# Decode attention over 65,536 keys: the last sixteen slots of V summed straight into the result, with idle matmuls ahead of the last piece

## The chip, the cores and the metric

The kernel runs on one core of one Trainium2 chip. The metric is the device time of one execution in microseconds (us). A profile is one traced execution. Its span is about 2 us shorter than the time of that execution (633.7 against 635.62 us in `before`).

## The reference, cut to what matters

```
q: [1, 32, 1, 128]   k, v: [1, 8, 65536, 128]   all bf16
scores = q . k^T * 128**-0.5        # each of the 8 heads of k and v serves 4 of q
p      = softmax(scores)            # over 65536 keys
out    = p . v                      # [1, 32, 1, 128]
```

K and V together are 268.4 MB and each element has to be read once, so the task is to read them.

## The kernel before: the parts that the change touches

The keys of one head are loaded in four steps of 4 MB. A step holds T = 128 *slots*: one slot is 128 keys, one on each partition, with 128 columns of V. The last step of the last head is loaded in five pieces, so that TensorE can begin on the first while the others are on their way:

```python
    CUTS = (T // 2, 3 * T // 4, 7 * T // 8, T - T // 16)     # 64, 96, 112, 120
    EDGE = CUTS[-1]                                          # 120
    # ... (v_step, collect and store: cut)
    def last_step(g, j):
        vt = load(v_view[g, j], "vt", CUTS)
        E = E_tiles.pop(g)
        Dp = psm.tile([P, D], fp32, name="Dp", tag="misc")
        nc.vector.memset(Dp[:, :], 0.0)

        def slot(t, dst, start, stop):
            i, c = t // CW, t % CW
            nc.tensor.matmul(
                out=dst, lhsT=E[:, j, c, i * HPG:(i + 1) * HPG],
                rhs=vt[:, t * D:(t + 1) * D], start=start, stop=stop,
            )

        ps_f = collect(g, False)
        for t in range(EDGE):
            s = t % NQ
            slot(t, Dp[s * QP:s * QP + HPG, :], t < NQ, t >= EDGE - NQ)
        Ds = stats.tile([P, D], fp32, name="Ds")
        nc.vector.tensor_copy(out=Ds[:, :], in_=Dp[:, :])
        for t in range(EDGE, T):
            slot(t, ps_f[:, :], False, False)
        nc.tensor.matmul(
            out=ps_f[:, :], lhsT=selh[:, :], rhs=Ds[:, :], start=False, stop=True
        )
        store(g, ps_f, nc.sync)       # scale by 1/sum on VectorE, then the output DMA
```

`vt` is the loaded part of V, `E` the exponentials of the scores, `HPG` the 4 rows of q that a head serves, and `Z`, below, a constant tile that holds q. There are two ways for a slot. Into `Dp`, four neighbouring slots go to four groups of partitions, and they overlap in the timeline below: eight take 0.28 us, where one takes 0.22 us. Into `ps_f`, the result itself, all go to the same 4 partitions and follow one another, 55 ns apart: eight take 0.61 us. What lies in `Dp` is copied (to `Ds`, 0.29 us on VectorE) and folded into the result by one fp32 matmul with `selh`, which the trace shows as two passes (`x2`, 0.38 us from the start of the first to the end of the second). Below, "piece 4" is slots 112 to 119, and "the last piece" is slots 120 to 127.

## Time and profile before

| | before |
|---|---|
| time, median of the first 3 runs | 635.18 us (635.05 to 635.27) |
| span of the profiled execution | 633.7 us |
| TensorE / VectorE busy | 59% / 54% |
| mean rate of DMA over the span | 424 GB/s |

The page of the profile of before, first its line of busy times, then from the table of 40 slices the share of DMA in tenths, then the chain of waits by engine:

```profile
PE 376.3 (59%) x2314; PEld 151.0 (24%) x2314; DVE 344.5 (54%) x342; ACT 21.7 (3%) x25; POOL 4.9 (1%) x7
...
DMA  9999999999999999999999999999999999999995
...
DMA 70%; PE 12%; DVE 9%; issue 7%; ACT 1%; ACTq 0%; DVEq 0%
```

DMA is busy in every slice but the last. No compute engine is busy for more than 59% of the span, and this change works behind the last landings only, so what it can gain lies there. The chain of waits from 600 us on (start, duration, what) shows how short that part is:

```profile
600.07 30.08 DMA vt<-in_v_dram
630.14 0.04 issue
630.19 0.61 PE ps_f L238 x8
630.79 0.23 PE ps_f L251 x2
631.02 0.03 issue
631.05 0.34 DVE o L225
```

The same stretch in the timeline (start, duration, engine, line, operation, output<-inputs, shapes, count, and in brackets the idle time before it and what ended it):

```profile
628.88 0.40 PE L238 MATMUL Dp<-vt,E 128*4 128x128 bf16 x16 [0.63 <-DMA vt<-in_v_dram]
...
629.55 0.28 PE L238 MATMUL Dp<-vt,E 128*4 128x128 bf16 x8 [0.28 <-DMA vt<-in_v_dram]
...
629.88 0.29 DVE L248 COPY Ds<-Dp 128x128 f32<-128x128 f32 x1 [5.30 <-PE Dp L238]
630.19 0.61 PE L238 MATMUL ps_f<-vt,E 128*4 128x128 bf16 x8 [0.36 <-DMA vt<-in_v_dram]
...
630.63 0.38 PE L251 MATMUL ps_f<-Ds,selh 128*4 128x128 f32 x2
631.05 0.34 DVE L225 TENSOR_SCALAR o<-ps_f,rl 4x128 bf16<-4x128 f32 x1 [0.88 <-PE ps_f L251]
```

Each group of slots waits for its own piece. Piece 4 lands at 629.55 and the last piece 0.64 us later. (I take the start of a piece's first slot for its landing; the chain puts the end of the DMA itself 0.04 us before it.) From there the path is: eight slots in a row, two passes of `selh`, the scaling. The yardstick is the time **from slot 112 (piece 4's landing) to the start of VectorE's scaling**. It is 1.50 us here (631.05 - 629.55).

### The profile page before, as it was taken

The page shows a single profiled execution, that of the slowest core. Times are in us where ns is not written, and L with a number is a line of the kernel's source. Part 1 is how long each engine was busy: PE and PEld are TensorE (multiplying, and loading weights), DVE is VectorE, ACT ScalarE, POOL GpSimd, SP SyncE. Part 2 cuts the span into 40 slices and gives each one's busy share as a digit, 9 for nine tenths or more (in the row PEclk, how much of TensorE's full clock was granted, in tenths as well). Part 3 has the DMA queues.
Part 4 walks back from the last instruction along what each step waited for, and adds up shares of the span by engine and source line. Part 5 has one row for each costly group of instructions (what it writes and reads, how often), then busy time and mean ns, then how long its engine had stood idle before and what let it go on. Part 6 is the DMA issues. An engine that isn't in the chain of part 4 may idle for free.

```text
span 633.7 us, 5456 instructions
## 1 busy us (share of the span) xinstructions
PE 376.3 (59%) x2314; PEld 151.0 (24%) x2314; DVE 344.5 (54%) x342; ACT 21.7 (3%) x25; POOL 4.9 (1%) x7
## 2 busy tenths in 40 slices
PE   0696846785457745477544775547664476644825
PEld 0232312231122311133211332113221132211313
DVE  0899834774338753376533765437554375553600
ACT  0000100010000000010000100001000010000100
POOL 3000000000000000000000000000000000000000
PEclk9999888877788967789677986779976799767867
DMA  9999999999999999999999999999999999999995
GB/s 366 430 429 429 430 435 434 429 430 435 431 429 432 430 429 430 433 434 431 431 432 427 430 432 430 429 430 434 429 431 429 432 429 430 431 432 432 429 424 232
DMA packets 10071, 268.82 MB, mean 424 GB/s; under 512 B 1344, under 2 KB 1344, under 8 KB 1728
## 3 DMA queue, kind: packets, MB, share of 16 engines
q1 hardware_dynamic: 9800, 268.44, 98.7%
q8 instruction: 18, 0.29, 0.2%
q10 hardware_dynamic: 248, 0.04, 0.0%
q14 instruction: 5, 0.04, 0.0%
HBM read 268.47 MB, written 0.01 MB: 424 GB/s over the span
## 4 chain that ended last, share of the span: by engine, by line
DMA 70%; PE 12%; DVE 9%; issue 7%; ACT 1%; ACTq 0%; DVEq 0%
DMA kt<-in_k_dram 56%; DMA vt<-in_v_dram 12%; PE S L136 8%; DVE kT L128 8%; DMA q_85<-in_q_dram 2%; DVE mx L147 1%; PE ps_f L216 1%; ACT ET L167 1%; PE A_1900 L200 0%; PE A_772 L200 0%; PE A_773 L200 0%; PE A_1901 L200 0%; DVE Z L112 0%; PE A_396 L200 0%; ACTq L77 0%
## 5 line engine op out<-in xcount | busy, mean ns | idle before, releaser
L136 PE MATMUL S<-kT,Z 128*128 128x512 bf16 x1024 | 283.9, 429 | 207.8 <-DVE kT L128 200.8
L128 DVE STREAM_TRANSPOSE kT<-kt 128x1024 int32<-128x1024 int32 x256 | 292.2, 1207 | 209.0 <-DMA kt<-in_k_dram 208.0
L136 PEld LDWEIGHTS <-Z 128*128 128x128 bf16 x1024 | 108.2, 106 | 381.5 <-issue 300.1
L200 PEld LDWEIGHTS <-E 128*32 128x32 bf16 x992 | 25.1, 100 | 49.4 <-issue 29.6
L167 ACT ACTIVATE ET<-S,nm 128x2048 bf16<-128x2048 f32 x8 | 15.7, 1967 | 575.2 <-DVE nm L164 575.2
L147 DVE TENSOR_REDUCE mx<-S 128x1 f32<-128x2048 f32 x8 | 18.3, 2292 | 10.4 <-PE S L136 10.4
L172 DVE STREAM_TRANSPOSE E<-ET 128x2048 bf16<-128x2048 bf16 x8 | 18.5, 2309 | 3.2 <-ACT ET L167 3.2
L200 PE MATMUL A_2977<-vt,E 128*32 128x512 bf16 x48 | 6.8, 544 | 13.6 <-DMA vt<-in_v_dram 13.6
L213 DVE COPY As_3088<-A_2978 128x512 f32<-128x512 f32 x1 | 0.7, 692 | 22.4 <-PE A_2978 L200 22.4
L149 PE MATMUL ps_t<-ident,mx 128*1 128x128 f32 x8 | 2.3, 283 | 16.9 <-DVE mx L147 16.9
L102 DVE STREAM_TRANSPOSE qT<-q_85 128x64 int32<-128x64 int32 x1 | 0.2, 246 | 16.4 <-DMA q_85<-in_q_dram 16.4
L200 PE MATMUL A_2652<-vt,E 128*32 128x512 bf16 x64 | 8.1, 426 | 0.0
L200 PE MATMUL A_2653<-vt,E 128*32 128x512 bf16 x64 | 7.9, 421 | 0.0
L200 PE MATMUL A_397<-vt,E 128*32 128x512 bf16 x64 | 7.4, 409 | 0.0
L175 PE MATMUL ps_l<-ls,selh 128*4 128x1 f32 x16 | 1.5, 165 | 9.9 <-ACT ET L167 9.9
L200 PE MATMUL A_396<-vt,E 128*32 128x512 bf16 x64 | 7.4, 401 | 0.0
L200 PE MATMUL A_2276<-vt,E 128*32 128x512 bf16 x64 | 7.0, 382 | 0.2 <-DMA vt<-in_v_dram 0.2
L200 PE MATMUL A_1148<-vt,E 128*32 128x512 bf16 x64 | 6.9, 382 | 0.0
L200 PE MATMUL A_1524<-vt,E 128*32 128x512 bf16 x64 | 6.9, 382 | 0.0
L200 PE MATMUL A_1900<-vt,E 128*32 128x512 bf16 x64 | 6.9, 382 | 0.0
L200 PE MATMUL A_772<-vt,E 128*32 128x512 bf16 x64 | 6.9, 382 | 0.0
L200 PE MATMUL A_2978<-vt,E 128*32 128x512 bf16 x48 | 6.9, 548 | 0.0
(95 smaller groups left out, 106.1 us busy)
## 6 DMA issues: line engine op xcount, KB each, us to landing
kt<-in_k_dram SPq DMA_DIRECT2D x32, 4096.0 KB, 46.1
vt<-in_v_dram SPq DMA_DIRECT2D x31, 4096.0 KB, 39.9
vt<-in_v_dram SPq DMA_DIRECT2D x1, 2048.0 KB
vt<-in_v_dram SPq DMA_DIRECT2D x1, 1024.0 KB
vt<-in_v_dram SPq DMA_DIRECT2D x1, 512.0 KB
vt<-in_v_dram SPq DMA_DIRECT2D x2, 256.0 KB
out_dram<-o ACTq DMA_DIRECT2D x7, 1.0 KB
q_85<-in_q_dram ACTq DMA_DIRECT2D x4, 8.0 KB, 6.5
```

The lines of the kernel that those rows point to most:

```text
L102: nc.vector.transpose(out=qT[:, :].bitcast(i32), in_=q4[:, :].bitcast(i32))
L128: nc.vector.transpose(out=kT[:, :].bitcast(i32), in_=kt[:, i * CW * D:(i + 1) * CW * D].bitcast(i32),)
L136: nc.tensor.matmul(out=S[:, j, :NCOL], lhsT=Z[:, b, e, g, w0:w0 + P], rhs=kT_v[:, b, e, :, :], start=(i == 0 and be == 0), stop=(i == NI - ...
L147: nc.vector.reduce_max(out=mx[:, :], in_=S[:, :, :NCOL], axis=AX.XY)
L149: nc.tensor.transpose(out=ps_t[:, :], in_=mx[:, :], identity=ident[:, :])
L167: nc.scalar.activation(out=ET[:, :].rearrange("p (a n) -> p a n", a=NQ), in_=S[:, :, :NCOL], func=ACT.Exp, bias=nm[:, :], scale=SCALE, acc ...
L172: nc.vector.transpose(out=E[:, :, :, :].rearrange("p a c r -> p (a c r)"), in_=ET[:, :])
L175: nc.tensor.matmul(out=ps_l[:, :], lhsT=selh[:, :], rhs=ls[:, :], start=True, stop=True)
L200: nc.tensor.matmul(out=A[u][s * QP:(s + 1) * QP, :], lhsT=E[:, j, c, :], rhs=vt_v[:, u, c, :, :], start=(j == 0 and c0 == 0), stop=(j == e ...
L213: nc.vector.tensor_copy(out=As[1][:, :, :].rearrange("p i d -> p (i d)"), in_=A[1][:, :])
L216: nc.tensor.matmul(out=ps_f[:, :], lhsT=sel[:, i * HPG:(i + 1) * HPG], rhs=As[i // HI][:, i % HI, :], start=(i == 0), stop=(stop and i == ...
```

## The change

Its intent: take the `selh` matmul out of the path behind the last landing. For that, the copy `Ds` has to come one piece sooner, so piece 4 goes straight into the result as well. Three idle matmuls, whose output nobody reads, are put where TensorE waits for the last piece, to keep it busy.

```diff
-    CUTS = (T // 2, 3 * T // 4, 7 * T // 8, T - T // 16)
-    EDGE = CUTS[-1]
+    CUTS = (T // 2, 3 * T // 4, 7 * T // 8, 15 * T // 16)    # the same numbers
+    EDGE = CUTS[-2]                                          # 112 instead of 120
 ...
+        W = psa.tile([P, 2 * D], fp32, name="W", tag="A0")
 ...
-        for t in range(EDGE, T):
+        def idle_work(n):
+            for _ in range(n):
+                nc.tensor.matmul(
+                    out=W[:, :], lhsT=Z[:, 0, 0, 0, :P],
+                    rhs=vt[:, (CUTS[-1] - 2) * D:CUTS[-1] * D], start=True, stop=True,
+                )
+
+        for t in range(EDGE, CUTS[-1]):
             slot(t, ps_f[:, :], False, False)
         nc.tensor.matmul(
-            out=ps_f[:, :], lhsT=selh[:, :], rhs=Ds[:, :], start=False, stop=True
+            out=ps_f[:, :], lhsT=selh[:, :], rhs=Ds[:, :], start=False, stop=False
         )
+        idle_work(3)
+        for t in range(CUTS[-1], T):
+            slot(t, ps_f[:, :], False, t == T - 1)
         store(g, ps_f, nc.sync)
```

The A tiles also get the tags that they already had by name, so that `W` can take the first one's place. (The comments after `#` are mine.)

More of the change, by code (lines that the diff above doesn't have):

```diff
@@ L189, in v_step @@
             A_tiles[g] = [
-                psa.tile([P, HI * D], fp32, name=f"A{u}") for u in range(2)
+                psa.tile([P, HI * D], fp32, name=f"A{u}", tag=f"A{u}") for u in range(2)
             ]
```

## The prediction

> **What bounds the kernel.** The DMA stream. The slice table shows DMA at 9 tenths or more in every slice but the last, 424 GB/s over the span, 268.44 MB; the chain of waits puts 70% of the span on DMA of K and V. In the last chain, DMA of V runs from 600.07 to 630.14 us; after it come only 0.61 us of eight matmuls on the last piece, 0.23 us of the two-pass selh matmul, a 0.34 us VectorE scaling at 631.05, and the output DMA issued at 631.42 (span 633.7). So the change can touch about 0.9 us of 635: 0.14%.
>
> **What changes.** The pieces of the load stay the same (120 = 15*128/16). Only TensorE's tail is reordered: slots 112 to 119 leave Dp for ps_f, the copy Ds moves ahead one piece, the selh matmul moves from behind the last piece to before it, and three 256-column idle matmuls stand between it and the last eight slots.
>
> **Costs, from the timeline of before (TensorE's granted clock was 1.00 from 628.8 to 631.1).**
> - Gap of two slots into ps_f: starts 630.19 to 630.52 in six steps, 55 ns. [...]
> - The selh matmul: two passes, 110 ns apart (630.63, 630.74), so about 0.22 us of TensorE's time. This leaves the path behind the last piece: the intended gain.
> - Slots 112 to 119 in Dp use four column groups (eight in 0.28 us, start to last end); in ps_f they follow one another at 55 ns: eight take about 0.44 us. That is 0.37 us more of TensorE's issue time before the last piece.
> - Ds: the 16 slots of the third piece end near 629.28, the copy takes 0.29 us, ready near 629.65: before selh needs it.
>
> **The sum.** Piece four released TensorE at 629.55, the last piece at 630.19. After: slots 112-119 issue from 629.55 to 629.99, selh to 630.21[...]. The last piece has then been there for about 0.35 us. The last eight slots start at about 630.54 and the last one at 630.93, with its end near 631.15 (218 ns each). Before, the last selh pass ended at 631.01. So the gain of 0.22 us is given back by 0.35 us of work standing in the way: the idle matmuls do not fill a wait, they overrun it. Net +0.1 us if the pieces land 0.64 us apart as here; -0.2 us if the last piece lands 0.4 us or more later. TensorE was already at clock 1.00 here, so warming buys nothing.
>
> **Predicted:** 635.2 us, 8 in 10 within 634.5 to 635.8. Faster by over 2%: 0.003; within 2%: 0.994; slower: 0.003.
>
> **What would show it.** DMA at 430 GB/s and the same landing times. The last eight slots not released by the DMA of V but by the PE queue (no idle time before them); TensorE's wait for the last piece, 0.36 us before, gone; VectorE's scaling at about 631.2 rather than 631.05. If the intent worked, the slots would idle until the DMA, and the scaling come 0.22 us sooner after it.
>
> **What would make it wrong.** Pieces landing further apart than in this one trace (then up to 0.2 us faster); the copy Ds or W's bank holding selh or the idle matmuls up; weight loads of the idle matmuls that are not hidden; or the whole DMA stream running differently in that program or session, which moves more than any of these terms.

The sum came to the last eight slots at about 630.54, 0.99 us after slot 112, and to net +0.1 us. The step from 630.21 (the end of `selh`) to 630.54 is the 0.33 us that it gave to the three idle matmuls. That was the estimate, and the 0.35 us, 630.93 and 631.15 that follow rest on it. `e2_idle24` later measured 0.110 us for each further idle matmul.

## The result, and the profile after

| | before | changed |
|---|---|---|
| median of 6 runs each | 635.43 us (635.05 to 635.85) | 635.56 us (635.27 to 635.79) |
| ratio | | 1.0001 (95% interval 0.9988 to 1.0014) |
| slot 112 to the scaling, first profile | 1.50 us | 1.84 us |

Ratios here are the mean time of one kernel's fast runs over that of the other's fast runs of the same rounds, so they are not quite the ratio of the medians. The time is the same. The profile shows that the two tails are not. Timeline of the changed kernel:

```profile
629.05 0.29 DVE L249 COPY Ds<-Dp 128x128 f32<-128x128 f32 x1 [4.74 <-PE Dp L238]
629.27 0.61 PE L238 MATMUL ps_f<-vt,E 128*4 128x128 bf16 x8 [0.28 <-DMA vt<-in_v_dram]
...
629.72 0.38 PE L259 MATMUL ps_f<-Ds,selh 128*4 128x128 f32 x2
...
630.03 0.50 PE L252 MATMUL W<-vt,Z 128*128 128x256 bf16 x3
...
630.46 0.61 PE L238 MATMUL ps_f<-vt,E 128*4 128x128 bf16 x8
631.11 0.34 DVE L225 TENSOR_SCALAR o<-ps_f,rl 4x128 bf16<-4x128 f32 x1 [1.77 <-PE ps_f L238]
```

And the chain of waits, in order of time:

```profile
629.27 0.61 PE ps_f L238 x8
629.88 0.22 PE ps_f L259 x2
630.10 0.43 PE W L252 x3
630.53 0.55 PE ps_f L238 x8
```

The last eight slots carry no bracket: TensorE did not idle before them, and no DMA released them. The chain that ended last runs through the idle matmuls. The last eight slots start 1.19 us after slot 112, where before they started after 0.64 us. The scaling, counted from piece 4, comes 0.34 us later than before. In absolute time it is only 0.06 us later (631.11 against 631.05), because piece 4 happened to land 0.28 us sooner in this execution.

### The profile page after: what moved, and what is told of

Same layout as the page of the kernel before. It is cut to its first block, busy times and chain, and to the rows that moved or that the text cites. A ratio compares the mean times of both kernels' runs of the same rounds, so it can differ in the third digit from the quotient of the medians.

```text
span 633.8 us, 5462 instructions
## 1 busy us (share of the span) xinstructions
PE 382.8 (60%) x2317; PEld 153.8 (24%) x2317; DVE 344.8 (54%) x342; ACT 21.7 (3%) x25; POOL 4.9 (1%) x7
## 4 chain that ended last, share of the span: by engine, by line
DMA 70%; PE 12%; DVE 10%; issue 7%; ACT 0%; SPq 0%; ACTq 0%; DVEq 0%
DMA kt<-in_k_dram 56%; DMA vt<-in_v_dram 12%; PE S L136 8%; DVE kT L128 8%; DMA q_85<-in_q_dram 2%; DVE mx L147 1%; PE A_396 L200 0%; PE A_397 L200 0%; PE A_773 L200 0%; DVE E L172 0%; PE A_772 L200 0%; ACT ET L167 0%; DVE Z L112 0%; SPq L72 0%; ACTq L77 0%
## 5 line engine op out<-in xcount | busy, mean ns | idle before, releaser
L136 PE MATMUL S<-kT,Z 128*128 128x512 bf16 x1024 | 289.8, 441 | 200.8 <-DVE kT L128 196.0
L136 PEld LDWEIGHTS <-Z 128*128 128x128 bf16 x1024 | 110.3, 108 | 378.2 <-issue 299.3
```

The lines of the kernel that those rows point to most:

```text
L136: nc.tensor.matmul(out=S[:, j, :NCOL], lhsT=Z[:, b, e, g, w0:w0 + P], rhs=kT_v[:, b, e, :, :], start=(i == 0 and be == 0), stop=(i == NI - ...
```

## The experiments

Two theories at the start. **A**: TensorE's order of work decides. The serial slots, `selh` and the idle matmuls together take longer than the 0.64 us between the last two landings, and the clock does not matter. **B**: the idle matmuls are of use, as they keep TensorE's clock up. A third possibility, **C**, was that the last piece simply landed late in the changed kernel's profile. The second profile of before brought a further theory, **W**, which comes below.

### The change without its idle matmuls (e1_idle0)

```diff
-        idle_work(3)
+        idle_work(0)
```

> The change without its three idle matmuls. Theory A (the idle matmuls and the serial slots overrun the last piece; the clock does not matter): from the first of slots 112-119 to VectorE's scaling, 1.50 us before and 1.84 us in the changed kernel, becomes 1.2 to 1.35 us; the last eight slots start 0.65 to 0.75 us after slot 112 instead of 1.19; the granted clock of 628 us on stays 1.00 and the slots follow at 55 ns. Rival B (the idle matmuls keep TensorE fast): the last slots follow at more than 55 ns and the clock is below 1.00. Rival C (the last piece simply landed late in the changed kernel's run): the last eight slots still start about 1.19 us after slot 112. Time: the same as before within 0.1%, since 0.2 us is 0.03%.

Measured: 635.33 us, ratio 0.9996 (0.9983 to 1.0008), correct. Timeline:

```profile
629.36 0.61 PE L238 MATMUL ps_f<-vt,E 128*4 128x128 bf16 x8 [0.28 <-DMA vt<-in_v_dram]
...
629.80 0.38 PE L259 MATMUL ps_f<-Ds,selh 128*4 128x128 f32 x2
...
630.02 0.61 PE L238 MATMUL ps_f<-vt,E 128*4 128x128 bf16 x8
630.67 0.34 DVE L225 TENSOR_SCALAR o<-ps_f,rl 4x128 bf16<-4x128 f32 x1 [1.25 <-PE ps_f L238]
```

The last slots start 0.66 us after slot 112, and the scaling 1.31 us after it: 0.19 us better than before and 0.53 us better than the change. That is the gain that was intended, and C falls. The granted clock was 1.00 here (628 to 632 us) without any idle matmul, which spoke against B in this execution.

### Twenty-four idle matmuls (e2_idle24)

```diff
-        idle_work(3)
+        idle_work(24)
```

> The change with 24 idle matmuls instead of 3. Theory A (they stand in TensorE's queue on the critical path): each adds its own spacing, about 0.115 us, so 21 more add about 2.4 us: the last eight slots start about 3.6 us after slot 112, and the time is 0.3 to 0.45% above before (about 637.6). If they only filled a wait, or if TensorE's tail were not on the path, the time would not move. Rival B (clock): no slower slots to be sped up, or less than 2.4 us because of a faster tail.

Measured: 638.06 us, ratio 1.0039 (1.0025 to 1.0053), the one difference that the times alone resolve. Timeline:

```profile
629.50 0.61 PE L238 MATMUL ps_f<-vt,E 128*4 128x128 bf16 x8 [0.27 <-DMA vt<-in_v_dram]
...
630.25 2.79 PE L252 MATMUL W<-vt,Z 128*128 128x256 bf16 x24
...
632.98 0.61 PE L238 MATMUL ps_f<-vt,E 128*4 128x128 bf16 x8
```

From the first idle matmul to the slots behind them are 2.73 us, where three took 0.43 us in the changed kernel (630.03 to 630.46). So the 21 more cost 2.30 us, 0.110 us each, and not the 0.115 that was expected. (The 0.115 was read off the changed kernel's trace: its first and third idle matmuls start at 630.03 and 630.26.) The last slots start 3.48 us after slot 112, 3.6 were expected. Idle matmuls in this place are on the path one for one.

### Idle matmuls alone, in the kernel before (e3_before_idle3)

```diff
+        for _ in range(3):          # between the slots of piece 4 and the last eight
+            nc.tensor.matmul(out=W[:, :], lhsT=Z[:, 0, 0, 0, :P],
+                             rhs=vt[:, (EDGE - 2) * D:EDGE * D], start=True, stop=True)
         for t in range(EDGE, T):
             slot(t, ps_f[:, :], False, False)
```

> The kernel before with three idle matmuls alone, between the Dp slots of the fourth piece and the last eight slots; selh stays at the end. Theory A: TensorE has about 0.55 us free there (0.64 us between the pieces less 0.08 us of issue), the three matmuls take 0.09 us of start and three times 0.115 us, 0.43 us, so the last slots start at the landing or at most 0.1 us late; from slot 112 to the scaling about 1.50 us as before (1.45 to 1.6). If idle matmuls cost what they take wherever they stand, 1.85 to 1.95 us. If they help by the clock, below 1.45 us.

(`W` and its tag come in as in the change. The 0.09 us of start is from the changed kernel's trace: two `selh` passes from 629.72 end at 629.94, and the first idle matmul starts at 630.03.) Measured: 635.41 us, ratio 0.9998 (0.9985 to 1.0012). Slot 112 starts at 629.16. Timeline:

```profile
629.37 0.50 PE L251 MATMUL W<-vt,Z 128*128 128x256 bf16 x3
...
629.80 0.61 PE L238 MATMUL ps_f<-vt,E 128*4 128x128 bf16 x8
...
630.67 0.34 DVE L225 TENSOR_SCALAR o<-ps_f,rl 4x128 bf16<-4x128 f32 x1 [0.89 <-PE ps_f L257]
```

The last slots start 0.64 us after slot 112, as before, and the scaling comes 1.51 us after it. In the order of before, the same three matmuls just fill the wait and cost nothing.

### The slots alone (e4_slots_only)

```diff
-    EDGE = CUTS[-1]
+    EDGE = CUTS[-2]        # piece 4 into the result; selh stays last, no idle matmuls
```

> The kernel before with only slots 112-119 moved to the result; selh still last and no idle matmuls. Theory A: these eight take 0.44 us of TensorE instead of 0.08, which still ends 0.2 us ahead of the last piece, so nothing changes after the landing: last eight slots released by the DMA of V about 0.64 us after slot 112, and slot 112 to scaling 1.50 us (1.45 to 1.55). If the serial slots alone cause the overrun, 1.7 us or more.

Measured in one look: 635.19 us. The chain of waits:

```profile
629.13 0.61 PE ps_f L238 x8
629.74 0.04 issue
629.78 0.61 PE ps_f L238 x8
630.38 0.23 PE ps_f L251 x2
```

The last slots started 0.65 us after slot 112, and the scaling came 1.51 us after it. Eight slots at 55 ns are issued in 0.44 us, so TensorE was free from about 629.57 and waited for the last piece, although the view names no releaser for so short a wait. The serial slots alone cost nothing either. So neither the slots nor the idle matmuls overrun the wait alone. The slots (0.44 us) and `selh` (0.22 us) just fill the 0.64 us (`e1_idle0`), and the idle matmuls were planned into a wait that those two had already used up.

### Narrow idle matmuls (e5_narrow3)

The prediction's sum left 0.33 us for three idle matmuls (630.21 to 630.54). In the changed kernel they took 0.52 us: 630.46 less the 629.94 at which two `selh` passes from 629.72 end. Three spacings of 0.11 us (`e2_idle24`) explain 0.33 of it. (The expectation below says 0.114 us, as it had spread an idle stretch at one edge of the group over the three.) This run tests where the other 0.19 us come from.

```diff
-                    out=W[:, :], lhsT=Z[:, 0, 0, 0, :P],
+                    out=W[:HPG, :], lhsT=Z[:, 0, 0, 0, :HPG],      # 4 weight columns, not 128
```

> The change with its three idle matmuls made narrow: 4 weight columns and 4 output partitions instead of 128, the same 256 columns of data. In the changed kernel the last slots start 0.52 us after the second selh pass's slot ends, where three spacings of 0.114 us account for 0.34; 0.09 us stands empty on each side of the group. Theory A1 (the gap is the change between a 128-column load and a 4-column load): both gaps go, the last slots start 0.98 to 1.04 us after slot 112 and the scaling 1.62 to 1.69 us after it. Theory A2 (the gaps are semaphore waits or a cost of any idle matmul): last slots at 1.19, scaling at 1.84 us, as in the changed kernel.

Measured in one look, 635.39 us:

```profile
629.53 0.38 PE L259 MATMUL ps_f<-Ds,selh 128*4 128x128 f32 x2
...
629.75 0.49 PE L252 MATMUL W<-vt,Z 128*4 128x256 bf16 x3
...
630.08 0.61 PE L238 MATMUL ps_f<-vt,E 128*4 128x128 bf16 x8
```

The three now take 0.33 us (629.75 to 630.08), both gaps are gone, the last slots start 0.99 us after slot 112 (629.09) and the scaling 1.64 us after it. The 0.19 us come with the 128-column loads in a stream of 4-column loads, about 0.1 us at each change of width. The edit narrows the loads and the output together, so the run does not part these two, nor does it tell what in the engine takes that time. The semaphore wait of the first idle matmul is ruled out, as it is there in both.

### Second profiles of the changed kernel and of before (e6_after_again, e7_before_again)

No edit in either.

> The changed kernel once more, for a second profile. From slot 112 to the last eight slots 1.19 us and to the scaling 1.84 us, within 0.03 us, if these are set by TensorE's order of work; they may differ by 0.1 us or more if they hang on when the pieces land. The moment at which slot 112 starts may differ by 0.3 us.

Measured: 1.19 and 1.83 us, as in the first profile. TensorE's order sets them.

> The kernel before once more, for a second profile. Fourth to last piece 0.64 us and slot 112 to scaling 1.50 us, within 0.05 us, if the landing of the last two pieces is as regular as the first five profiles suggest; the start of slot 112 may lie anywhere from 629.1 to 629.6 us.

Measured: the landings were as regular as expected (0.64 us), but slot 112 to the scaling took **1.91 us** instead of 1.50. Timeline of this second profile of before:

```profile
629.49 0.28 PE L238 MATMUL Dp<-vt,E 128*4 128x128 bf16 x8 [0.28 <-DMA vt<-in_v_dram]
...
630.13 0.81 PE L238 MATMUL ps_f<-vt,E 128*4 128x128 bf16 x8 [0.36 <-DMA vt<-in_v_dram]
...
630.73 0.64 PE L251 MATMUL ps_f<-Ds,selh 128*4 128x128 f32 x2
631.40 0.34 DVE L225 TENSOR_SCALAR o<-ps_f,rl 4x128 bf16<-4x128 f32 x1 [1.29 <-PE ps_f L251]
```

The eight slots took 0.81 us instead of 0.61, and `selh` 0.64 instead of 0.38. The granted clock fell in the middle of them. Stretches of 3.41 us (columns: stretch, its length, busy time and count of TensorE, weight loads, VectorE, ScalarE and GpSimd, then the granted clock, the share of DMA, GB/s):

```profile
626.98:630.39 3.41, 1.55 (x61) 1.11 (x61) 0.29 (x1) 0.00 (x0) 0.00 (x0) 1.00 0.20 73
630.39:633.80 3.41, 0.97 (x9) 0.47 (x5) 0.34 (x1) 0.00 (x0) 0.00 (x0) 0.50 0.00 0
```

At 630.39, in the middle of the last slots, the clock fell to half, after a stretch of 3.41 us in which TensorE was busy for 1.55 us and had no gap over 0.65 us. In this execution there was something for idle matmuls to save, and the prediction's "warming buys nothing" does not hold for it.

### Theory W, taken from all traces

The clock records of the traces show two levels, 0.50 and 1.00, and a grid of changes. In the first profiles of before and of the changed kernel, every span of constant clock (52 and 56 of them), but the last that is cut off, is a whole multiple of 3.413 us long: 3.413, 6.827, 10.240 and so on up to 37.547. In all fourteen traces the stretches of such a grid, but the last where it is cut off, read 0.50 or 1.00. I call such a stretch a window, laid the grid on each trace and counted what followed:

| TensorE busy in a window of 3.41 us | at full clock: next full / next half | at half clock: next full / next half |
|---|---|---|
| under 1.3 us | 0 / 310 | 0 / 384 |
| 1.3 to 1.9 us | 86 / 65 | 0 / 58 |
| 1.9 to 2.5 us | 187 / 0 | 0 / 60 |
| 2.5 to 2.9 us | 150 / 0 | 39 / 35 |
| 2.9 us and more | 775 / 0 | 336 / 2 |

A recount on the clock's own records, to the nanosecond, moves the cells by at most a dozen and leaves every zero. In it, the windows that could go either way at full clock held 1.39 to 1.84 us.

So in these traces half clock followed every full-clock window with under 1.3 us busy (310 of 310) and none with 1.9 us or more (0 of 1112). Full clock followed none of the 502 half-clock windows with under 2.5 us busy, and 336 of the 338 with 2.9 us or more. These counts are all that W rests on, and nothing here says that they hold beyond this case. In the tail, the danger is a window that ends between about 629.5 and 631 us. I slid such a window over the traces in steps of 0.1 us, for ends from 629.2 to 631.1. The busy time of before went down to 1.74 us in its first profile and to 1.48 us in its second, inside the range where these traces show either outcome. In the three profiles of the changed kernel it stayed at 1.97, 2.14 and 2.49 us or more, above it. By W, whether the clock falls in an execution of before then depends on where the grid happens to lie. In its first profile it fell too, but only at 631.54, half a us after the scaling had begun. The matching window of the changed kernel's first profile:

```profile
627.62:631.04 3.42, 2.51 (x65) 1.62 (x49) 0.29 (x1) 0.00 (x0) 0.00 (x0) 1.00 0.10 32
```

The times of before fit. All 35, with those of the two profiled executions, fall into two groups: 23 from 635.05 to 635.62 (mean 635.37) and 12 from 635.78 to 635.98 (mean 635.93). The profiled execution with the fallen clock took 635.96. The versions of the change without idle matmuls in the last wait (`e1_idle0` and two more below) gave 15 times, all from 635.02 to 635.66, where a third of them in an upper group would have been five. That the whole upper group is due to the clock is an inference: one traced execution of before lies in it. The rival is a late landing. In the fourteen traces the time is 4.55 to 4.68 us more than the start of the scaling. So a time of 635.78 with a tail of 1.50 us would need slot 112 at 629.60 or later, and in the thirteen traces where it starts at the landing it was never later than 629.55. That makes the rival less likely, but does not exclude it.

### Smaller last pieces (e8_small_last)

```diff
-    CUTS = (T // 2, 3 * T // 4, 7 * T // 8, 15 * T // 16)
-    EDGE = CUTS[-2]
+    CUTS = (T // 2, 3 * T // 4, 7 * T // 8, 15 * T // 16, 31 * T // 32)
+    EDGE = 13 * T // 16      # copy Ds after slot 103; selh right after slot 111; idle_work(0)
```

> A candidate: no idle matmuls; the copy Ds taken after slot 103, so that selh is done before the fourth piece lands; the last piece split in two of 4 slots each, which leaves four serial slots behind the last landing. Measured from the first slot of the third piece (slot 96), the scaling starts at 2.17 us before, 2.51 in the changed kernel, 1.98 without idle matmuls. If the last landing does not move (about 1.31 us after slot 96), this gives about 1.85 to 1.90. If an additional piece makes the last landing later, 1.98 or more. Time: same as before within 0.1%; not resolvable by the clock on the wall, only by the profile.

Measured: 635.29 us, ratio 0.9996 (0.9982 to 1.0010), and 1.99 us from slot 96 to the scaling (628.54 to 630.53), against 1.98 without idle matmuls. A miss: nothing was gained over `e1_idle0`. The trace shows `selh` waiting for the copy until 629.22 and the last 16 slots then following one another from 629.44 with no idle time between them. The tail had become a matter of TensorE's work, so a smaller last piece had nothing to shorten. Whether the last landing moved cannot be seen, as nothing waited for it.

### Less work in the kernel before (e9_before_cut)

```diff
         for t in range(EDGE):
+            if CUTS[0] <= t < CUTS[1]:
+                continue             # slots 64 to 95 left out: wrong result on purpose
             s = t % NQ
```

> The kernel before with slots 64 to 95 left out (32 matmuls fewer behind the second piece; wrong result on purpose). All loads, and all work behind the last two pieces, stay. A new theory, W (the second profile of before made it): the granted clock is decided at the ends of windows of 3.41 us on a grid; a window at full clock in which TensorE was busy less than about 1.6 us is followed by half clock; when such an end falls into the tail, the last slots and selh run at half clock, and the scaling comes about 0.4 us later (9 of 25 times of before lie at 635.78 to 635.98, the others at 635.05 to 635.62). The left-out slots were 0.62 us of busy time, so windows that end from 629.6 to 631.5 fall to 1.1 to 1.5 us: the clock drops in most executions. Theory W: slower than before although it does less: most times at 635.75 to 636.2, the profile with clock 0.5 before the scaling and 1.85 to 2.05 us from slot 112 to the scaling. Theory A (only the work behind the last piece counts): 1.50 us and times as before, 635.05 to 635.98 with a third above 635.7.

(The 3.41 us is the grid of the traces above. The 1.6 us was the estimate: in the tails, 1.55 us in `e7_before_again` and 1.62 us in `before` were followed by half clock, 1.80 us in `e1_idle0` by full clock.)

Measured: five times, 635.16 to 635.31 and 635.96 (the profiled one); ratio 0.9995 (0.9981 to 1.0008). In the profiled execution:

```profile
629.29 0.28 PE L238 MATMUL Dp<-vt,E 128*4 128x128 bf16 x8 [0.27 <-DMA vt<-in_v_dram]
...
629.93 1.01 PE L238 MATMUL ps_f<-vt,E 128*4 128x128 bf16 x8 [0.36 <-DMA vt<-in_v_dram]
...
631.41 0.34 DVE L225 TENSOR_SCALAR o<-ps_f,rl 4x128 bf16<-4x128 f32 x1 [1.49 <-PE ps_f L253]
```

with these windows:

```profile
626.25:629.66 3.41, 1.03 (x43) 0.61 (x33) 0.04 (x1) 0.00 (x0) 0.00 (x0) 1.00 0.32 120
629.66:633.07 3.41, 1.44 (x10) 0.94 (x9) 0.59 (x2) 0.00 (x0) 0.00 (x0) 0.50 0.00 0
```

The clock did what W says: 1.03 us of work in the window, half clock from its end, 2.12 us from slot 112 to the scaling. The frequency is not what I expected of W: one of five, not most. Sliding the window over this trace gives under 1.3 us for ends from 629.2 to 630.5, 1.3 us of a grid of 3.41, so "most" was more than W itself says; but one of five is too few to say more. The experiment supports how the clock falls and says nothing of how often.

### The cut, with idle matmuls in its place (e10_cut_idle5)

```diff
+            if t == CUTS[0]:
+                idle_work(5)         # short for the same matmul, on data of piece 2
             if CUTS[0] <= t < CUTS[1]:
                 continue
```

> The same cut, and five idle matmuls in the place of the 32 slots, in the wait for the third piece, not for the last (wrong result too). Theory W: about 0.8 us of busy time comes back where nothing waits for it, the clock stays 1.00 until after the scaling, 1.50 us from slot 112 to the scaling, and the times are those of before without its upper group: 635.0 to 635.6. Theory A or a drop for another reason: as the cut without idle matmuls.

Measured: 635.15, 635.31, 635.36, 635.52 and 636.18; ratio 0.9999 (0.9986 to 1.0011); the result is wrong on purpose, as in the run before. The profiled execution kept its clock (1.51 us from slot 112 to the scaling), but one time lies in the upper range, which I had not expected. My sum was at fault: the five idle matmuls show 0.72 us busy in the trace, the 32 slots that they replace 0.62 us, so this kernel is hardly safer than before, and before is in the upper group one time in three. Inconclusive.

### Idle matmuls one wait earlier (e11_idle4_earlier)

```diff
         for t in range(EDGE):
+            if t == CUTS[1]:
+                idle_work(4)         # short for the same matmul, on data of piece 2
 ...
-        idle_work(3)
+        idle_work(0)
```

> The version that should beat both: the change without idle matmuls in the last wait, and four of them in the wait for the third piece, between slots 95 and 96, where TensorE sits idle 0.6 us anyway (4 x 0.114 + 0.2 = 0.66 us, a little late at worst). Slot 112 to scaling 1.31 us, clock 1.00 throughout, times 635.0 to 635.5 with none above 635.65, mean 0.2 to 0.35 us under before and 0.3 to 0.5 us under the change.

Measured: 635.31 us (635.24 to 635.66), ratio 0.9997 (0.9984 to 1.0009), correct. Timeline:

```profile
628.09 0.61 PE L248 MATMUL W<-vt,Z 128*128 128x256 bf16 x4
...
628.79 0.40 PE L238 MATMUL Dp<-vt,E 128*4 128x128 bf16 x16
...
629.46 0.61 PE L238 MATMUL ps_f<-vt,E 128*4 128x128 bf16 x8 [0.28 <-DMA vt<-in_v_dram]
...
630.77 0.34 DVE L225 TENSOR_SCALAR o<-ps_f,rl 4x128 bf16<-4x128 f32 x1 [1.24 <-PE ps_f L238]
```

1.31 us, as without any idle matmuls, and the busy time of a sliding window did not go under 2.68 us in this trace for ends up to 631.1. This version has the short tail and the most margin for the clock. Its five times average 635.36, 0.2 us under the mean of all times of before (635.56) and 0.27 us under that of the change (635.63), where 0.3 to 0.5 was expected; one of them (635.66) is a hair above the bound that I had set. It is the better version by its trace. By its times it is the same as before.

### The changed kernel a third time (e12_after_third)

No edit.

> The changed kernel once more, for its distribution of times. Theory W: its windows hold 1.97 us of busy time or more whichever way the grid falls (before: down to 1.74 in the first profile's phase, 1.48 in the second's), so the clock stays 1.00 and there is one group only, about 0.34 us above the lower group of before: 635.3 to 635.85, 1.84 us from slot 112 to the scaling. Against that, were the clock to drop in it as well, some times at 636.0 or more.

Measured: 635.57 to 635.96, median 635.72; ratio 1.0003 (0.9990 to 1.0015). 1.83 us from slot 112 to the scaling, clock 1.00. The highest time lies 0.11 us above the stated range. The changed kernel has 12 times, mean 635.63, with no gap between two groups. None of its three traces shows the clock falling.

## Why the prediction was right or wrong, point by point

- **The time**: 635.2 us predicted (634.5 to 635.8), 635.56 measured; the chance of "within 2%" was rightly put at 0.994. The reason given was right: the DMA stream ends where it ends, and the change works on less than 1 us behind it. But the range is 1.3 us wide and the tails differ by 0.34 us, so the time says nothing for or against the sum; the traces do.
- **The pieces of the sum**: `selh` 0.22 us predicted, 0.22 us measured in `e1_idle0` (629.80 to 630.02). Serial slots 0.44 us predicted, 0.45 measured (629.27 to 629.72). The gap of 0.64 us between the last landings came back in every profile in which TensorE waited for both.
- **The overrun**: the prediction said that the idle matmuls would not fill a wait but overrun it, that the last slots would have no idle time before them, and that TensorE's wait for the last piece would be gone. All three stand in the trace. `e3_before_idle3` and `e4_slots_only` show that neither the idle matmuls nor the slots overrun the wait alone, and `e1_idle0` that the slots and `selh` together just fill it. The slots and the idle matmuls without `selh` were not run; by their sizes (0.44 and 0.52 us) they would overrun it too.
- **The mis-sized term**: the three idle matmuls, to which the sum gave 0.33 us (630.21 to 630.54). Measured 0.52 us. Three spacings of 0.110 us (`e2_idle24`) make up 0.33 of it; the other 0.19 us are what `e5_narrow3` ties to the changes between 128-column and 4-column weight loads. With narrow ones the last slots start at 0.99 us, the prediction's own number. The prediction had named weight loads that are not hidden as a way to be wrong. So the net in the tail is +0.34 us, not "+0.1 us".
- **The wrong step**: "TensorE was already at clock 1.00 here, so warming buys nothing." That was read from one execution. In another one of the same kernel the clock fell 0.26 us after the last slots began, and the tail took 0.41 us longer (1.91 against 1.50).
- **The account**: against the lower group of before (mean 635.37) the changed kernel's mean (635.63) is 0.26 us worse, near the 0.34 us of the tails. Against all times of before (635.56) it is 0.07 us worse, as the upper group, a third of the executions, pays about as much in another way. Nothing in this account reaches 0.1% of the time.

What stays open: how often the clock falls in before (12 of 35 times in the upper group, by inference from one traced execution in it), why the cut kernel was in that range only once in five, and which part of the change keeps the clock up. The serial slots (0.61 us busy for eight, against 0.28 in `Dp`) add busy time as well as the idle matmuls. With the slots alone (`e4_slots_only`), the slots and `selh` (`e1_idle0`) and the idle matmuls alone (`e3_before_idle3`) a sliding window went down to 1.80, 1.79 and 1.84 us, where the table allows either outcome.

## What to carry to other kernels

Before filling a wait, add up everything that has been moved into it: here two moved parts used it up, and each further matmul of the filler pushed the path out by its own 0.11 us (`e2_idle24`). If the filler is there for the clock, put it into an earlier wait that has room: four idle matmuls between slots 95 and 96 left the tail at 1.31 us and a sliding window of 3.41 us busy for 2.68 us or more, at clock 1.00 (`e11_idle4_earlier`). That the place inside a window does not matter was not tested by itself. For effects far below the spread of the times, compare traces from a fixed event, and take more than one trace: before's clock at 631 us was 1.00 in its first profile and 0.50 in its second (`e7_before_again`).
